# Top-32 attention with two expert layers on one Trainium2 core: transposes and weighted sums of attention weights moved one step later

## Chip, cores and metric

One core of one Trainium2 chip runs the whole program. The metric is device time in microseconds (us). Engines: TensorE (PE; its weight loads PEld), VectorE (DVE), ScalarE (ACT), GpSimd (POOL), and SyncE (SP), whose queue issues most DMAs.

## The reference

Attention over 4 batches, 8 heads, 576 positions, 64 channels keeps the 32 largest scores of each row; its output feeds a gated layer and then a layer of 8 experts, of which each token takes one.

```python
scores = scale * np.matmul(q, k.transpose(0, 1, 3, 2))
kth = np.partition(scores, -top_k, axis=-1)[..., -top_k:-top_k + 1]
scores = np.where(scores >= kth, scores, -1000000000.0)
attn = np.exp(scores - np.max(scores, axis=-1, keepdims=True))
attn = attn / (np.sum(attn, axis=-1, keepdims=True) + 1e-09)
x = np.matmul(attn, v)                       # then to (2304, 512)
h = x @ w_in;  x = (h * np.clip(h + 3, 0, 6) / 6) @ w_out
# each token: expert = argmax(x @ w_gate), weight = its softmax
out[mask] = gate_w[mask, None] * (np.maximum(xe @ w1[e], 0.0) @ w2[e])
```

## The kernel before

The work of attention is cut into T = 144 tiles of up to 128 query rows of one head. Two heads form a pair (p); a visit is the rows of one part of a batch (b) for one pair. A full tile is (head, j); two of them, head 0 and head 1 of the same rows, share a buffer of exponentials. Where a part ends with 64 rows, both heads' 64 rows make one short tile "T", with a buffer of its own; there are 16.

One loop runs over steps t = 0 to T + 5. Each step works on several tiles at once, each at another stage:

- `qk(t + LA)` and `sevac(t + LA)`: scores into PSUM (sps) and their copy by ScalarE into one of five `sbuf`.
- `top_a(t)`: VectorE finds the 32 largest of each row, by maxima of eight blocks (cd), then rounds of maxima (m) and replacements (cw).
- `top_c(t - 1)`, `act_exp(t - 1)`, `act_sign(t - 1)`, `top_z(t - 1)`: the exponentials on ScalarE into `pbuf[pairs[t] % NPB]` (NPB = 2), a count by signs (jk, sg), and a masked copy of the scores (z) on VectorE.
- `mask(t - 2)`: a maximum of z (L646), the match j (L650) that gives the threshold, then the multiplication of the exponentials with the mask (L654, "the mask" below). For a short tile GpSimd then moves and clears columns (L246, L659, L660).
- `trans(t - 3)`, `tevac(t - 3)`: TensorE transposes the masked weights into the PSUM tile `ptps` (L670; the fifth, of the last 64 positions of both heads, L672), ScalarE copies them to SBUF (L248, pt), with one buffer for head 0 (pta, PTA = 1) and one for head 1 and short tiles (ptb, PTB = 1).
- `pv(t - 4)`, `xevac(t - 4)`: TensorE multiplies with the values (L704), also into `ptps`, once for the two heads; VectorE inverts the sums of weights (rs, L717), ScalarE scales (xp, L722). A step later `xt` transposes the result for the next layer (L740, xh, xl). When the last one of a block of 256 rows is done, `blkready` rises.
- `moe_step()`: one of 16 steps of a block in the gated layer (a gated step), if its block is ready: products of layer one (l1ps, L778), gf on ScalarE and VectorE (L784, L790), gh and gl on GpSimd, sums of layer two (yps, L809). `gate_step()` works off the choice of experts of a finished block; its matmuls and a read of counts (lex, L869) use `ptps` too. Conversions of the weights are spread over the first 35 steps or so.

The order on each engine is made by a planner: an instruction gets the due time `pr0 + PRIO[name]` in force when it was written, pr0 rises by STEP = 400 a step, and among those whose inputs the planner's own clock has ready the earliest due goes first. Dependences follow the order of writing; accesses to one PSUM tile by different engines are kept in that order even where their columns differ. Of use here, each within a step: pv −40, qk 10, trans 210, l2 260, l1 310, xevac 440, tevac 450, mask 55, match 560, exp −295, load −1940. The tile `ptps` also holds the small tables `psum_isum`, which the match reads, and `psum_iota`. Loads of values (`load_v`) for visit n + 2 are written once the sums of visit n are, and go through SP's queue.

Behind the loop the remaining steps of the gated layer run alone; then the second expert layer follows, weights streamed from memory.

Of the kernel before, what the change touches and what calls it, by code (L numbers as in the profile page):

```python
# [28 lines left out]
AGE = 0  # L29
KB = 1  # L30
LA = 2
PTA = 1
PTB = 1
SPOOL = 0
TPOOL = 0
WPOOL = 0
# [12 lines left out]
    tevac=450, xt1=-1170, l2=260, sign=175, epi_c=1010, wo=1175, prep=105, top8=270, rounds=-815, epi_b=165, l1=310,  # L49
# [5 lines left out]
def attention_two_moe_kernel(  # L55
# [64 lines left out]
    T = len(tiles)  # L120
# [4 lines left out]
    NV = len(visits)  # L125
    vlast = {n: t for t, (n, o) in enumerate(tiles)}
# [8 lines left out]
    def pr(name):  # L135
        tc.cur_priority = max(0, pr0[0] + PRIO[name])

    def run(gen):
        for _ in gen:
            pass  # L140
# [54 lines left out]
    def body(cs, exact):  # L195
# [45 lines left out]
        def mod(t, n):  # L241
            return (t * n) % 16 < n

        def copy(pool, dst, src):
            if pool:
                G.tensor_scalar(dst, src, 1.0, 0.0, op0=ALU.mult, op1=ALU.add)  # L246
            else:
                A.activation(dst, src, AF.Copy)  # L248
# [83 lines left out]
        conv_load()  # L332


        NPB, NSB, VB = 2, 3 + LA, 2


        pbuf = [ap1.tile([P, 2 * S], F32, name=f"pbuf{i}") for i in range(NPB)]
# [25 lines left out]
        kdone, qdone, kloaded, qloaded, vloaded = [0], [0], [0], [0], [0]  # L364


        def rows(h):
            return slice(h * D, (h + 1) * D)
# [76 lines left out]
        def loads(t):  # L445
            pr("load")
            while kloaded[0] < len(kjobs) and kloaded[0] < kdone[0] + KB + (pjob[0] is not None and pjob[0][0] == "k"):
                b, p = kjobs[kloaded[0]]
                kn = ap1.tile([P, NFC, 2, D], F32, tag="kn", bufs=KB, name=f"kn{b}_{p}")
                kt_ = ap1.tile([TAIL, 2, D], F32, tag="kt", bufs=KB, name=f"kt{b}_{p}")  # L450
                for h in range(2):
                    s = k[b, 2 * p + h]
                    SP.dma_start(kn[:, :, h, :], mains(s))
                    SP.dma_start(kt_[:, h, :], s[N4:S, :])
                kraw[b, p] = (kn, kt_)
                kage[kloaded[0]] = t
                kloaded[0] += 1
            while qloaded[0] < NV and qloaded[0] <= qdone[0] and (pjob[0] is None or pjob[0][0] != "q"):
                n = qloaded[0]
                b, p, q0, w, first = visits[n]  # L460
                qraw[n] = ap1.tile([P, 2, 2, 2, D], F32, tag="qn", bufs=1, name=f"qn{n}")
                nf = w // P
                for h in range(2):
                    s = q[b, 2 * p + h]
                    for j in range(nf):
                        SP.dma_start(qraw[n][:, j, h],
                                     s[q0 + j * P:q0 + (j + 1) * P, :].unsqueeze(1).to_broadcast([P, 2, D]))
                    if w % P:
                        SP.dma_start(qraw[n][0:TAIL, nf, h],
                                     s[q0 + nf * P:q0 + w, :].unsqueeze(1).to_broadcast([TAIL, 2, D]))  # L470
                qage[qloaded[0]] = t
                qloaded[0] += 1

        def load_v():
            pr("load")
            n = vloaded[0]
            vbuf[n] = (vtile[n % VB], vtail[n % VB])
            for h in range(2):
                s = v[visits[n][0], 2 * visits[n][1] + h]
                SP.dma_start(vbuf[n][0][:, h, :, 0:D], mains(s))  # L480
                SP.dma_start(vbuf[n][1][h * TAIL:(h + 1) * TAIL, h, 0:D], s[N4:S, :])
            vloaded[0] += 1
# [181 lines left out]
        def trans(t):  # L664
            pr("trans")
            pb = ts[t]["pb"]
            o = tiles[t][1]
            c0 = SW if o != "T" and o[0] else 0
            for c in range(NFC):
                PE.transpose(ptps[:, c * P:(c + 1) * P], pb[:, c0 + c * P:c0 + (c + 1) * P], ident)  # L670
            if o == "T" or o[0]:
                PE.transpose(ptps[:, N4:SW], pb[:, N4:SW], ident)  # L672

        def tevac(t):
            pr("tevac")
            d = ts[t]
            o = tiles[t][1]
            if o == "T" or o[0]:
                d["pt"] = ap1.tile([P, SW], F32, tag="ptb", bufs=PTB, name=f"pt{t}")
                copy(mod(t, TPOOL), d["pt"], ptps[:, 0:SW])  # L680
            else:
                d["pt"] = ap1.tile([P, N4], F32, tag="pta", bufs=PTA, name=f"pt{t}")
                copy(mod(t, TPOOL), d["pt"], ptps[:, 0:N4])


        def pv(t):
            n, o = tiles[t]
            if o != "T" and o[0] == 0:
                return
            pr("pv")  # L690
            pt = ts[t]["pt"]
            vn, vp = vbuf[n]
            x2 = xps.rearrange("p (h d) -> p h d", h=2)
            mm = [(x2, pt[:, N4:SW], vp)]
            for c in range(NFC):
                cs_ = slice(c * P, (c + 1) * P)
                if o == "T":
                    mm.append((x2, pt[:, cs_], vn[:, :, c, :]))
                else:
                    mm.append((x2[:, 0, :], ts[t - 1]["pt"][:, cs_], vn[:, 0, c, :]))  # L700
            if o != "T":
                mm += [(x2[:, 1, :], pt[:, c * P:(c + 1) * P], vn[:, 1, c, :]) for c in range(NFC)]
            for i, (d_, a_, b_) in enumerate(mm):
                PE.matmul(d_, a_, b_, start=(i == 0), stop=(i == len(mm) - 1))  # L704

        xp = {}
        xtq = []
        blkready = [0]

        def xevac(t):  # L710
            n, o = tiles[t]
            if o != "T" and o[0] == 0:
                return
            pr("xevac")
            x2 = xps.rearrange("p (h d) -> p h d", h=2)
            r = ap1.tile([P, 2], F32, tag="rs", bufs=2, name=f"rs{t}")
            V.tensor_scalar(r, x2[:, :, D], 1e-9, None, op0=ALU.add)  # L717
            V.reciprocal(r, r)
            j = o if o == "T" else o[1]
            xp[n, j] = ap1.tile([P, P], F32, tag="xp", bufs=2, name=f"xp{n}_{j}")  # L720
            for h in range(2):
                A.activation(xp[n, j][:, rows(h)], x2[:, h, 0:D], AF.Copy, scale=r[:, h:h + 1])  # L722
            del ts[t]
            if o != "T":
                del ts[t - 1]
            xtq.append((n, j, t))
            if t == vlast[n]:
                del vbuf[n]
# [236 lines left out]
        def pfin():  # L965
            pnext()
            yield
# [20 lines left out]
            qk(t)  # L988
            sevac(t)
        cacc = 0  # L990
        for t in range(T + 6):
            pr0[0] = pbase + t * STEP
            loads(t)
            while vloaded[0] < NV and (vloaded[0] < VB or vlast[vloaded[0] - VB] <= t - 5):
                load_v()
            ms = moe_step()
            next(ms, None)
            if 0 <= t - 3 < T:
                trans(t - 3)
            if 0 <= t - 1 < T:  # L1000
                top_c(t - 1)
                act_exp(t - 1)
            if t + LA < T:
                ensure(t + LA)
                qk(t + LA)
            if 0 <= t - 4 < T:
                pv(t - 4)
            if t + LA < T:
                sevac(t + LA)
            if 0 <= t - 4 < T:  # L1010
                xevac(t - 4)
            xg = None
            if xtq and (xtq[0][2] < t - 4 or t >= T):
                xg = xt(*xtq.pop(0))
                next(xg)
            if 0 <= t - 3 < T:
                tevac(t - 3)
            if xg:
                next(xg)
            next(ms, None)  # L1020
            if 0 <= t - 1 < T:
                act_sign(t - 1)
            next(ms, None)
            pj = t < T and xg is None and pstart(t + LA)
            if pj:
                pnext()
                if pjob[0] is not None:
                    pnext()
            cacc += CRATE
            others = [ms, mask(t - 2)]  # L1030
            while cacc >= 16:
                cacc -= 16
                others.append(conv_next())
            if xg:
                others.append(xg)
            if pj and pjob[0] is not None:
                others.append(pfin())
            if t < T:
                top_a(t, chain(*others))
            else:  # L1040
                run(chain(*others))
            if 0 <= t - 1 < T:
                top_z(t - 1)
            gate_step()
# [239 lines left out]
```

## Time and profile before

| | us |
|---|---|
| median of 3 runs | 1306.36 (1302.1 to 1306.69) |
| the profiled execution | 1308.57 |
| its span, first to last instruction | 1306.4 |
| busy: TensorE, weight loads | 1168.6, 1034.4 |
| busy: VectorE | 975.4 |
| busy: ScalarE, GpSimd | 820.6, 344.1 |
| mean granted clock of TensorE | 0.941 |

Busy times are shares of an average over unlike stages: loop steps with weight conversions, loop steps with the gated layer, the gated layer alone, the second expert layer. What a change in the loop is worth is read in the stage where it lies, from the waits there. Matmuls are pipelined, so a busy TensorE is not one at its peak.

### The profile page before, as it was taken

The page shows a single profiled execution, that of the slowest core. Times are in us where ns is not written, and L with a number is a line of the kernel's source. Part 1 is how long each engine was busy: PE and PEld are TensorE (multiplying, and loading weights), DVE is VectorE, ACT ScalarE, POOL GpSimd, SP SyncE. Part 2 cuts the span into 40 slices and gives each one's busy share as a digit, 9 for nine tenths or more (in the row PEclk, how much of TensorE's full clock was granted, in tenths as well). Part 3 has the DMA queues.
Part 4 walks back from the last instruction along what each step waited for, and adds up shares of the span by engine and source line. Part 5 has one row for each costly group of instructions (what it writes and reads, how often), then busy time and mean ns, then how long its engine had stood idle before and what let it go on. Part 6 is the DMA issues. An engine that isn't in the chain of part 4 may idle for free.

```text
span 1306.4 us, 23615 instructions
## 1 busy us (share of the span) xinstructions
PE 1168.6 (89%) x7253; PEld 1034.4 (79%) x7253; DVE 975.4 (75%) x3882; ACT 820.6 (63%) x2087; POOL 344.1 (26%) x578
## 2 busy tenths in 40 slices
PE   4577688899999999999999899999985999999995
PEld 3466576788889988888878789898874899999894
DVE  5999999988898999998998798999432444444420
ACT  4777867767688777777777677787432444444421
POOL 1232345421232321221322222322343122222100
PEclk9985589989899999999999899999997999999998
DMA  5444465544444555543543354644684455455400
GB/s 139 132 134 134 122 205 188 166 150 121 130 118 121 140 154 143 135 133 105 128 138 100 92 146 126 135 124 131 217 245 126 135 171 169 152 170 162 135 19 25
DMA packets 184664, 180.20 MB, mean 138 GB/s; under 512 B 123933, under 2 KB 148813, under 8 KB 184528
## 3 DMA queue, kind: packets, MB, share of 16 engines
q1 hardware_dynamic: 180112, 167.52, 44.6%
q0 software_dynamic: 4416, 11.08, 2.6%
q8 instruction: 60, 0.98, 0.3%
q14 instruction: 76, 0.62, 0.2%
HBM read 160.52 MB, written 19.59 MB: 138 GB/s over the span
## 4 chain that ended last, share of the span: by engine, by line
PE 61%; DVE 23%; ACT 8%; DMA 3%; issue 3%; SPq 1%; POOL 1%; ACTq 0%; POOLq 0%; DVEq 0%
PE l1ps L778 10%; PE lp L1119 10%; PE ops L1136 10%; PE yps L809 9%; PE ptps L704 9%; DVE pbuf L654 4%; PE sps L556 4%; PE ptps L670 4%; DVE z L619 3%; DVE cd L586 3%; DVE z L646 3%; DVE m L592 2%; DVE cw L597 2%; ACT pt L248 1%; PE ptps L837 1%
## 5 line engine op out<-in xcount | busy, mean ns | idle before, releaser
L809 PE MATMUL yps<-wo,gh 128*128 128x512 f32 x576 | 214.0, 416 | 3.9 <-DMA wo<-wod 3.4
L778 PE MATMUL l1ps<-xh,wih 128*128 128x256 f32 x576 | 174.1, 302 | 15.5 <-DVE gf L790 12.6
L586 DVE MAX8 cd<-sbuf 128x8 f32<-128x72 f32 x1152 | 183.8, 218 | 2.3 <-ACT sbuf L248 1.9
L246 POOL TENSOR_SCALAR gh<-gf 128x256 fp32r<-128x256 f32 x144 | 64.9, 450 | 414.0 <-DVE gf L790 170.1
L778 PE MATMUL l1ps<-xl,wih 128*128 128x256 f32 x576 | 167.5, 291 | 0.0
L778 PE MATMUL l1ps<-xh,wil 128*128 128x256 f32 x576 | 167.3, 290 | 0.0
L704 PE MATMUL ptps<-vn,pt 128*128 128x65 f32 (+1 forms) x1152 | 156.8, 294 | 0.0
L704 PEld LDWEIGHTS ptps<-vn,pt 128*128 128x128 f32 x1152 | 154.0, 214 | 0.0
L927 DVE TENSOR_TENSOR wl<-raw,wh 128x1024 fp32r<-128x1024 f32 x64 | 78.7, 1233 | 98.1 <-ACT wh L926 98.1
L670 PE MATMUL ptps<-ident,pbuf 128*128 128x128 f32 x576 | 99.3, 297 | 40.2 <-DVE pbuf L654 30.3
L778 PEld LDWEIGHTS l1ps<-xh,wih 128*128 128x128 f32 x576 | 113.0, 196 | 26.6 <-DVE gf L790 19.9
L619 DVE SCALAR_TENSOR_TENSOR z<-sbuf,uall 128x576 f32<-128x576 f32 x144 | 132.9, 923 | 0.4 <-ACT uall L610 0.4
L654 DVE SCALAR_TENSOR_TENSOR pbuf<-sbuf,tall,pbuf 128x576 f32<-128x576 f32 x144 | 124.9, 868 | 0.1
L809 PEld LDWEIGHTS yps<-wo,gh 128*128 128x128 f32 x576 | 108.7, 192 | 19.5 <-issue 4.5
L670 PEld LDWEIGHTS ptps<-ident,pbuf 128*128 128x128 f32 x576 | 70.5, 151 | 65.9 <-ACT jk L636 14.3
L926 ACT ACTIVATE wh<-raw 128x1024 fp32r<-128x1024 f32 x64 | 67.6, 1060 | 87.2 <-PE lp L1119 38.2
L627 ACT ACTIVATE pbuf<-sbuf,nb 128x576 f32<-128x576 f32 x144 | 110.9, 773 | 17.9 <-PE ptps L672 15.9
L809 PE MATMUL yps<-wo,gl 128*128 128x512 f32 x288 | 118.6, 412 | 0.8 <-POOL gl L798 0.8
L784 ACT ACTIVATE gf<-l1ps,three 128x256 f32<-128x256 f32 x144 | 68.1, 473 | 75.4 <-PE l1ps L778 63.9
L778 PEld LDWEIGHTS l1ps<-xl,wih 128*128 128x128 f32 x576 | 113.1, 196 | 2.7
L636 ACT ACTIVATE jk<-sbuf,uall 128x576 bf16<-128x576 f32 x144 | 111.9, 777 | 3.2
L778 PEld LDWEIGHTS l1ps<-xh,wil 128*128 128x128 f32 x576 | 113.2, 196 | 0.1
(178 smaller groups left out, 2957.3 us busy)
## 6 DMA issues: line engine op xcount, KB each, us to landing
wo<-wod SPq DMA_DIRECT2D x144, 512.0 KB
raw<-in_moe_w_dram SPq DMA_DIRECT2D x64, 512.0 KB
vn<-in_v_dram SPq DMA_DIRECT2D x96, 128.0 KB
rawi<-in_moe_w_in_dram SPq DMA_DIRECT2D x16, 512.0 KB
rawo<-in_moe_w_out_dram SPq DMA_DIRECT2D x16, 512.0 KB
qn<-in_q_dram SPq DMA_DIRECT2D x128, 64.0 KB
wod<-wc SPq DMA_DIRECT2D x16, 512.0 KB
yd<-y SPq DMA_DIRECT2D x18, 258.0 KB
```

Source lines behind the costliest of these rows:

```text
L586: V.max(cd[:, c, :], s[:, c * CK:(c + 1) * CK])
L619: V.scalar_tensor_tensor(d["z"], s, d["u"], s, op0=ALU.is_le, op1=ALU.mult)
L627: A.activation(d["p"], d["s"], AF.Exp, bias=d["nb"], scale=SCALE)
L636: A.activation(jk, d["s"][:, 0:S], AF.Sign, bias=ts[t]["u"], scale=-1.0, accum_out=d["sg"])
L654: V.scalar_tensor_tensor(d["p"], d["s"], tall[:, t:t + 1], d["p"], op0=ALU.is_ge, op1=ALU.mult)
L670: PE.transpose(ptps[:, c * P:(c + 1) * P], pb[:, c0 + c * P:c0 + (c + 1) * P], ident)
L704: PE.matmul(d_, a_, b_, start=(i == 0), stop=(i == len(mm) - 1))
L778: PE.matmul(dst, a[:, c, fs], b_[:, c, :], start=(n == 0), stop=(n == 3 * NCC - 1))
L809: PE.matmul(yps[tt], a[:, tsl], b_, start=(f == 0 and m == 0), stop=(f == NF1 - 1 and m == 2))
L927: V.tensor_tensor(l, raw, r_(h), op=ALU.subtract)
L1119: PE.matmul(lp, a[:, c, fs], b_[:, c, :], start=(n == 0), stop=(n == 3 * NCC - 1))
L1136: PE.matmul(ops_[j], a[:, js], b_[:, ns], start=(f == 0 and m == 0), stop=(f == NF2 - 1 and m == 2))
```

## The change

Transposes and weighted sums of a tile are written one step later: `trans` and `tevac` work on tile t − 4, `pv` and `xevac` on t − 5. Due times within a step are the same. The loop has one more turn. The loads of values and the transposes of results (`xt`) follow by one step. There are three buffers of exponentials and two of each kind of transposed weights.

```diff
-PTA = 1
-PTB = 1
+PTA = 2
+PTB = 2
...
-        NPB, NSB, VB = 2, 3 + LA, 2
+        NPB, NSB, VB = 3, 3 + LA, 2
...
-        for t in range(T + 6):
+        for t in range(T + 7):
             pr0[0] = pbase + t * STEP
             loads(t)
-            while vloaded[0] < NV and (vloaded[0] < VB or vlast[vloaded[0] - VB] <= t - 5):
+            while vloaded[0] < NV and (vloaded[0] < VB or vlast[vloaded[0] - VB] <= t - 6):
                 load_v()
             ms = moe_step()
             next(ms, None)
-            if 0 <= t - 3 < T:
-                trans(t - 3)
+            if 0 <= t - 4 < T:
+                trans(t - 4)
             if 0 <= t - 1 < T:
                 top_c(t - 1)
                 act_exp(t - 1)
             if t + LA < T:
                 ensure(t + LA)
                 qk(t + LA)
-            if 0 <= t - 4 < T:
-                pv(t - 4)
+            if 0 <= t - 5 < T:
+                pv(t - 5)
             if t + LA < T:
                 sevac(t + LA)
-            if 0 <= t - 4 < T:
-                xevac(t - 4)
+            if 0 <= t - 5 < T:
+                xevac(t - 5)
             xg = None
-            if xtq and (xtq[0][2] < t - 4 or t >= T):
+            if xtq and (xtq[0][2] < t - 5 or t >= T):
                 xg = xt(*xtq.pop(0))
                 next(xg)
-            if 0 <= t - 3 < T:
-                tevac(t - 3)
+            if 0 <= t - 4 < T:
+                tevac(t - 4)
```

## Rows read from the trace of the kernel before

**Rows 1.** Busy us by stage: PE, PEld, DVE, ACT, POOL; granted clock, DMA share, GB/s.
```profile
0.00:160.00 160.00, 96.86 (x390) 79.80 (x391) 140.06 (x539) 110.27 (x276) 43.27 (x58) 0.78 0.47 134
160.00:276.00 116.00, 99.40 (x604) 84.49 (x605) 106.37 (x396) 80.42 (x214) 52.76 (x76) 0.90 0.55 172
276.00:916.00 640.00, 614.30 (x4336) 549.91 (x4335) 580.55 (x2693) 484.88 (x1364) 161.54 (x319) 0.98 0.47 129
```

**Rows 2.** The same view, instructions of line 619 (z, one a tile) on DVE alone.
```profile
276.00:916.00 640.00, 90.77 (x109) 0.98 0.47 129
765.00:916.00 151.00, 23.66 (x28) 1.00 0.47 126
```

**Rows 3.** Busy us as in rows 1, of two other stretches.
```profile
765.00:916.00 151.00, 148.77 (x1086) 135.26 (x1085) 137.92 (x646) 115.51 (x319) 40.11 (x68) 1.00 0.47 126
1100.00:1200.00 100.00, 100.00 (x518) 90.51 (x518) 44.31 (x54) 43.77 (x63) 20.03 (x27) 1.00 0.51 160
```

**Rows 4.** Time line, 820 to 822 us: start, us, engine, line, out<-in [idle before <-releaser].
```profile
820.19 0.23 DVE L650 SCALAR_TENSOR_TENSOR j<-ptps,sg,z 128x16 f32<-128x16 f32 x1 [0.33 <-ACT pt L248]
...
820.47 0.82 DVE L654 SCALAR_TENSOR_TENSOR pbuf<-sbuf,tall,pbuf 128x576 f32<-128x576 f32 x1
...
821.43 0.63 PE L670 MATMUL ptps<-ident,pbuf 128*128 128x128 f32 x4
...
821.90 0.39 PE L704 MATMUL ptps<-vp,pt 128*128 128x130 f32 x2
```

**Rows 5.** Busy us by stage, instructions of line 790 (gf) on DVE alone.
```profile
160.00:276.00 116.00, 6.16 (x15) 0.90 0.55 172
...
920.00:985.00 65.00, 7.08 (x17) 0.97 0.78 238
```

**Rows 6.** Waits of PE, 276 to 916 us: who waited for whom: us, times, longest.
```profile
PE ptps L670 <- DVE pbuf L654: 5.2, 15, 0.7
PE ptps L670 <- DVE lex L869: 4.5, 4, 1.9
PE ptps L672 <- DMA qn<-in_q_dram: 3.2, 1, 3.2
...
PE ptps L672 <- POOL pbuf L659: 0.9, 1, 0.9
```

**Rows 7.** Time line around one short tile, 734 to 739 us.
```profile
734.00 0.24 POOL L246 TENSOR_SCALAR pbuf<-pbuf 64x64 f32<-64x64 f32 x1 [4.37 <-DMA td<-tok,ad]
...
734.51 0.47 PE L672 MATMUL ptps<-ident,pbuf 128*128 128x128 f32 x1 [3.24 <-DMA qn<-in_q_dram]
...
738.76 0.16 DVE L717 TENSOR_SCALAR rs<-ptps 128x2 f32<-128x2 f32 x1 [6.19 <-PE ptps L704]
```

**Rows 8.** Busy us as in rows 1, the two stretches behind it.
```profile
735.00:740.00 5.00, 5.00 (x22) 4.71 (x22) 1.24 (x7) 2.31 (x6) 0.14 (x1) 0.50 0.02 5
740.00:745.00 5.00, 5.00 (x24) 4.58 (x22) 3.24 (x15) 1.97 (x7) 1.52 (x4) 0.63 0.33 105
```

**Rows 9.** Waits of PE, 0 to 160 us.
```profile
PE ptps L670 <- DVE pbuf L654: 25.2, 12, 4.9
```

**Rows 10.** Waits of DVE, 0 to 160 us and 160 to 276 us.
```profile
DVE rs L717 <- PE ptps L704: 2.9, 2, 1.4
...
DVE rs L717 <- PE ptps L704: 3.6, 2, 2.0
```

**Rows 11.** Waits of all engines, 276 to 916 us.
```profile
POOL pbuf L660 <- PE ptps L672: 15.6, 8, 6.1
ACT pbuf L627 <- PE ptps L672: 10.6, 15, 3.6
DVE j L650 <- ACT pt L248: 7.2, 22, 0.6
```

**Rows 12.** Waits of SP's DMA queue, 276 to 916 us.
```profile
SPq L764 <- PE yps L809: 212.6, 71, 8.9
...
SPq L481 <- PE ptps L704: 31.1, 22, 5.1
```

## Prediction

> **What bounds the kernel now.** I read first the busy time of each engine stage by stage [rows 1], with the number of tiles [rows 2]. Up to 160 us tiles pass without steps of the gated layer (gated steps below); VectorE is busy 140.06 of 160 us, TensorE 96.86, so VectorE sets the pace. From 160 to 276 us they carry the last weight conversions and the first of those steps: VectorE 92%. From 276 to 916 us 109 tiles pass with one such step each, 5.87 us a tile; here both are close to full, TensorE 614.30 of 640 us and VectorE 580.55. Behind 916 us there is no attention left. The change acts on the first three stages and, by one more loop turn, on the fourth; the expert layer behind it, up to the end of the span, it doesn't touch.
>
> In the third stage TensorE idles 640 − 614.30 = 25.7 us, and its granted clock is 0.98, which costs about another 13 us. This is all that TensorE could ever give back there. In the stretch from 765 to 916 us, where hardly a stall is left, 28 tiles take 151 us, 5.39 each [rows 2, 3]: the floor that the stage has when nothing goes wrong.
>
> By the busy share of matmuls TensorE is at 98.5% in that stretch, by that of weight loads at 89.6%; from 1100 to 1200 us, where matmuls never pause (100.00 of 100 us), the weight loads stand at 90.5% [rows 3]. So 89.6% is as full as this engine gets here. The Trainium skill ("Perfetto Trace Analysis", Identifying the Most-Contended Engine) says that matmul occupancy is no good measure of the room left and that the busy share of weight loads is one; read so, a tenth of the stage would be free, and the third rival below is what would follow.
>
> Then the waits. Which wait does the change aim at? In step t the transposes are those of tile t−3, the mask is that of t−2: a tile's transposes come one step after its mask. One pass in the time line [rows 4]: the match (j) starts at 820.19 us, released by the copy of transposed weights (pt), the mask at 820.47, the transposes at 821.43, and the weighted sum is queued right behind them. So each step holds a ring: transposes, copy, match, mask, transposes of the next tile.
>
> **The change part by part.** No operation is added or removed; the 144 tiles keep their transposes, copies and sums. What moves is when they may start.
>
> *(a) One more loop turn.* The gated steps of a block start when its last weighted sum is transposed, so all start one turn later, and the loop has T+7 turns. One turn in the VectorE-bound stages loses its gated step, worth 0.41 us of VectorE there (6.16 us for 15 multiplications of gf); one more turn with a gated step alone is run behind the attention: 65 us for 17 of them, 3.8 us [rows 5]. Sum +3.4 us. Ends: 0, if that turn fits into idle time behind 916 us; 7.7 us, a whole turn of the second stage (116 us for 15 of them).
>
> *(b) TensorE's waits in the third stage.* The transposes wait for the mask 15 times, 5.2 us in all, and for GpSimd's part of the mask of a short tile (T) in 2 places, 3.2 and 0.9 us [rows 6]. The 3.2 us carry a DMA's name, but the time line shows what it was [rows 7]: GpSimd stood 4.37 us behind an indirect DMA of its own, copied the short tile's columns only at 734.00 us, and the fifth transpose started at 734.51. The granted clock then stood at 0.50 (1.2 GHz throughout) and 0.63 in the next two stretches of 5 us [rows 8], so some 4.3 us more were lost, and VectorE too stood still for 6.19 us, for the sum behind the transpose. With a whole step (5.9 us) between mask and transposes both kinds of wait go. I count the event in full, 3.2 + 4.3 + 0.9 = 8.4 us, as no engine worked through it; the mask's 5.2 us I count by half, 2.6, since VectorE at 91% is next in line. Sum −11.0 us. Ends: −13.6 (all) and 0 (VectorE takes everything back).
>
> *(c) The first two stages.* Here the transposes wait for the mask 25.2 us in 12 places [rows 9]; that is worth nothing itself, since VectorE is the bound and TensorE has 63 us free there [rows 1]. What counts is that VectorE waits for the weighted sums that are queued behind: 2.9 + 3.6 us [rows 10]. A sum no longer held behind the mask comes up to a step earlier in relation to it; I take half, −3 us, as the engine does other work meanwhile only in part. Ends −6.5 and 0.
>
> *(d) Three buffers of exponentials.* An exponential is written over those of two pairs before, once they are transposed; ScalarE waits 10.6 us for those transposes in the third stage, GpSimd 15.6 us for the clearing of a short tile's columns [rows 11]. With three buffers and transposes a step later, an even tile's exponential needs transposes issued two steps before it instead of one. Both waits shrink. ScalarE is 76% busy and GpSimd 25% [rows 1], so I take 0; ends −10.6 and 0.
>
> *(e) Two buffers of each kind of transposed weights.* With the sums as many steps behind the copies as before, the second buffer lets a copy go ahead of the sum that still reads the first; that is a wait of a copy for a sum, and the views of waits have none. 0; as an upper end the whole of ScalarE's wait before the exponentials, which (d) holds already.
>
> *(f) Loads.* The values of visit n+2 are asked for one step later, as are the sums that free their buffer and those that need them; the distance stays. On SP's queue these loads (31.1 us of waiting for sums before those of the tail rows) move past one load of second-layer weights (wo), and wo waits 212.6 us for its own buffers in this stage, 3.0 us each time [rows 12]: what passes was waiting anyway. 0; if that cover failed in one place, TensorE would stand for one such wait, 3.0 us.
>
> *(g) What stays in the ring.* The match reads a table that shares a PSUM tile with the transposes: it waits for the copy 22 times, 7.2 us in the third stage [rows 11]; the transposes wait for another VectorE read of it (lex, a gate's) 4 times, 4.5 us [rows 6]. These orders hold after the change too: transposes, copy, match, transposes. Only the mask (0.82 us in the pass above) leaves the ring; match, copy and transposes stay [rows 4]. As transposes arrive earlier at that point, more of them will meet lex or the match: I take half of the 4.5 us once more, +2.3; ends 0 and what the second rival makes of it.
>
> Sum: 3.4 − 11.0 − 3.0 + 2.3 = −8.3 us. The profiled execution took 1308.57 us (span 1306.4), 2.2 above the median of the runs; the difference is taken to that median, 1306.36: 1298.1, so **1298 us**, with 1291 to 1301 as its own range.
>
> **The rivals.** *First, the gain stays small:* VectorE is the next bound, 5.3 us of work a tile (580.55/109) against 5.87 us [rows 1, 2], and the ring through the PSUM tile still closes once a step. Then only half of (b)'s event comes back, 4 us, against +3.4: about 1305 us. For it speaks that the mask's waits in stage three are short, 0.35 us on average, and that the big one is a single event. The Trainium skill ("PSUM — Partial Sum Buffer", PSUM bank collisions raise a hardware error) says that two engines must not touch one bank at once, reads against reads included, so such an order of copy and match has to be kept; the 22 waits agree.
>
> *Second, slower:* the order of each engine's instructions is made anew by due times. Transposes are due at 210, ahead of the sums of layer two (260) and the products of layer one (310). Until now they were held back by the mask and those matmuls went first. Now nothing but the match or lex holds them, so they can be set ahead of that work, and at run time TensorE, which is in order, waits for VectorE with it queued behind. At the mean of today's waits, 0.35 us, at every second tile that is 54 × 0.35 = 19 us: about 1317 us. It decides from 8.3/109 = 0.08 us a tile. Against it: before, the same place costs only 0.05 us a tile (5.2/109).
>
> *Third, a larger gain:* it is the ring and not the engines that sets 5.87 us a tile, and with 0.82 us out of it half of TensorE's 25.7 + 13 us comes back instead of (b)'s 11: 1298 − 8 = 1290, down to 1280 if more does. Against it stands the clean stretch, 5.39 us a tile with the ring as it is.
>
> **How the numbers follow.** Forecast 0.38, first rival 0.31, second 0.20, third 0.11. The forecast's own range holds its bounds of (a) to (c) near the middle; for 8 in 10 the range goes from 1284 (most of the third) to 1315 (most of the second). About 0.5%, 6.5 us, is what a measurement can tell from no change: below 1299.8 lie the third rival and most of the forecast, 0.46; between, the first and the forecast's edge, 0.35; above 1312.9 the second, 0.19.
>
> **What would show it.** Right: no wait of transposes for the mask and none for GpSimd's clearing; ScalarE's wait before the exponentials near 0; gated steps starting some 7 us later; one more lone gated step, 3 to 4 us, behind the attention; 109 tiles in 630 us or less. Wrong: as much waiting of the transposes for the match or lex as there was for the mask (second rival); VectorE's busy share in the third stage over 95% with no gain (first); a stage of 620 us or less (third).

## The result and the profile after

The changed kernel takes 1293.5 us (1290.71 to 1293.98 in 5 runs) against 1306.36 (1301.7 to 1309.84): a ratio of 0.9891 [0.9864, 0.9918], 12.9 us less where 8.3 were forecast. The profiled spans, 1290.9 and 1306.4, differ by 15.5. A second comparison gave 0.9905 (e12, below).

After, busy time by the stages of [rows 1], same columns; the stages now end a little earlier:

```profile
0.00:160.00 160.00, 87.25 (x386) 71.59 (x387) 144.65 (x541) 109.86 (x274) 41.51 (x58) 0.85 0.47 130
160.00:276.00 116.00, 101.48 (x634) 88.61 (x632) 112.05 (x428) 87.33 (x231) 53.21 (x78) 0.89 0.61 193
276.00:916.00 640.00, 620.17 (x4446) 554.14 (x4446) 578.34 (x2686) 486.79 (x1365) 171.09 (x328) 1.00 0.48 132
```

In the third stretch the granted clock is 1.00 where it was 0.98. But fixed stretches no longer hold the same work, so from here on I cut by tiles: from the start of one z (line 619) to that of another, 20 and 35 being its number. The first stage is then z0 to z20, the second z20 to z35, the third z35 to z143, and behind z143 stand the last gated steps. In us:

| | z0–z20 | z20–z35 | z35–z143 | z143 to the last gf | gf behind z143 |
|---|---|---|---|---|---|
| before | 135.5 | 114.7 | 638.9 | 72.2 | 21 |
| before, second profile (e11) | 134.5 | 114.2 | 637.6 | 71.5 | 21 |
| after | 135.3 | 105.0 | 624.0 | 81.6 | 22 |
| after, second profile (e12) | 135.3 | 105.0 | 623.4 | 81.3 | 22 |

The two profiles of each kernel agree within 1.5 us in every stage. They are two executions each, though: other executions of the kernel before went from 1295.1 to 1310.7 us on one chip, so a few us of a stage can be the execution's own. Between the first two profiles the gain is 9.7 us in the second stage and 14.9 in the third, and 9.4 are given back behind the attention; expert layer and first stage stay.

Before, the second and the third stage, cut by tiles (columns as in rows 1):

```profile
162.00:276.70 114.70, 98.10 (x602) 83.19 (x601) 104.70 (x393) 79.16 (x213) 52.15 (x75) 0.90 0.56 175
276.71:915.61 638.90, 613.20 (x4325) 548.81 (x4325) 579.82 (x2692) 484.37 (x1361) 161.40 (x318) 0.98 0.47 129
```

After, the same two:

```profile
161.40:266.40 105.00, 91.05 (x562) 79.19 (x561) 102.24 (x390) 78.10 (x209) 50.83 (x74) 0.88 0.60 190
266.37:890.34 623.97, 603.68 (x4330) 539.35 (x4330) 576.44 (x2688) 485.42 (x1361) 163.06 (x317) 1.00 0.49 132
```

In the second stage VectorE's work is nearly the same (104.70 and 102.24 us); its idle time falls from 10.0 us to 2.8. In the third the number of matmuls is the same (4325, 4330), but two things fell: TensorE's idle time from 638.90 − 613.20 = 25.7 us to 20.3, and its *busy* time from 613.20 to 603.68. With equal work, less busy time goes here with a higher granted clock, 1.00 against 0.98. So of the 14.9 us I count 9.5 as clock and 5.4 as waits.

The waits after, beside [rows 6, 11] (who waited for whom: us, times, longest), TensorE first, then all engines, 276 to 916 us:

```profile
PE ptps L670 <- DVE lex L869: 4.4, 5, 2.0
PE ptps L670 <- DVE j L650: 1.9, 5, 0.6
...
POOL pbuf L660 <- PE ptps L672: 18.0, 7, 5.5
DVE j L650 <- ACT pt L248: 13.1, 28, 1.0
...
ACT pbuf L627 <- PE ptps L672: 2.3, 5, 0.6
```

No transposes wait for the mask (pbuf, L654) or for GpSimd's clearing any more. ScalarE's wait ahead of the exponentials went from 10.6 to 2.3 us. GpSimd's wait for its clearing did not shrink (15.6, now 18.0) and costs nothing. The transposes wait 6.3 us for lex and the match, 4.5 before, and the match's wait for the copy grew from 7.2 to 13.1 us. Of VectorE's wait for the sums (rs, L717), 17.4 us before in the third stage cut by tiles, 1.6 are left.

### The profile page after: what moved, and what is told of

The parts are those of the page before. It is cut to its first block, busy times and chain, and to the rows that moved or that the text cites. A ratio compares the mean times of both kernels' runs of the same rounds, so it can differ in the third digit from the quotient of the medians.

```text
span 1290.9 us, 23533 instructions
## 1 busy us (share of the span) xinstructions
PE 1148.2 (89%) x7253; PEld 1017.9 (79%) x7253; DVE 976.0 (76%) x3882; ACT 821.9 (64%) x2087; POOL 345.8 (27%) x578
## 4 chain that ended last, share of the span: by engine, by line
PE 60%; DVE 9%; ACT 4%; DMA 3%; issue 2%; POOL 0%; SPq 0%; POOLq 0%; ACTq 0%; DVEq 0%
PE l1ps L778 11%; PE lp L1119 10%; PE ops L1136 10%; PE yps L809 10%; PE ptps L704 7%; PE sps L556 4%; PE ptps L670 3%; DVE pbuf L654 1%; DVE cd L586 1%; PE ptps L837 1%; DVE z L646 1%; PE tp L1101 1%; DVE z L619 1%; DVE cw L597 1%; PE misc L414 1%
## 5 line engine op out<-in xcount | busy, mean ns | idle before, releaser
L809 PE MATMUL yps<-wo,gh 128*128 128x512 f32 x576 | 209.6, 411 | 1.2 <-DMA wo<-wod 0.8
L704 PE MATMUL ptps<-vn,pt 128*128 128x65 f32 (+1 forms) x1152 | 146.6, 282 | 0.0
L704 PEld LDWEIGHTS ptps<-vn,pt 128*128 128x128 f32 x1152 | 143.4, 201 | 0.0
L654 DVE SCALAR_TENSOR_TENSOR pbuf<-sbuf,tall,pbuf 128x576 f32<-128x576 f32 x144 | 126.2, 877 | 0.1
L670 PE MATMUL ptps<-ident,pbuf 128*128 128x128 f32 x576 | 97.9, 295 | 21.5 <-DVE j L650 14.9
L248 ACT ACTIVATE sbuf<-sps 128x576 f32<-128x576 f32 x144 | 93.1, 647 | 37.2 <-PE sps L556 22.1
L798 POOL TENSOR_TENSOR gl<-gf,gh 128x256 fp32r<-128x256 f32 x144 | 112.5, 782 | 11.4
```

Of the source, the lines that this page charges most:

```text
L654: V.scalar_tensor_tensor(d["p"], d["s"], tall[:, t:t + 1], d["p"], op0=ALU.is_ge, op1=ALU.mult)
L798: G.tensor_tensor(gl, gf, r_(gh), op=ALU.subtract)
L809: PE.matmul(yps[tt], a[:, tsl], b_, start=(f == 0 and m == 0), stop=(f == NF1 - 1 and m == 2))
```

## The experiments

Ratios are to the kernel before on the same chip, with 95% intervals. None of the versions is faster than the change beyond the noise. Stage lengths of a version come from one profile of it.

**The buffers alone** (e1), and **the change without the second buffers of transposed weights** (e2):

```diff
-PTA = 1
-PTB = 1
+PTA = 2
+PTB = 2
...
-        NPB, NSB, VB = 2, 3 + LA, 2
+        NPB, NSB, VB = 3, 3 + LA, 2
```

e2 is the changed kernel with PTA = PTB = 1.

> Three buffers of exponentials and two of each kind of transposed weights, but transposes and sums at their old steps. Theory (the gain is that the transposes no longer stand behind the mask): nothing of that changes, so 1306 +- 4 us, with ScalarE's wait before the exponentials (L627, 10.6 us in the third stage before, 2.3 after) near 0 and VectorE's wait for the sums (rs, 17.4 us) as before. Rival (the gain comes from the buffers): 1296 us or less, rs waits down to some 5 us.

> The change with single buffers of transposed weights (three of exponentials). Theory: the second buffers do nothing, since a copy comes behind the sum that read the buffer anyway: 1293 +- 4 us. Rival (they carry part of the gain, by letting a copy go ahead of a sum): 1300 us or more, and copies (pt, L248) that wait for sums (L704).

e1: 1305.87 us, 1.0001 [0.9978, 1.0023]. e2: 1292.0 us, 0.9894 [0.9864, 0.9924], the change's own ratio. Buffers without later steps bring nothing: in e1 ScalarE's wait ahead of the exponentials falls from 10.6 to 2.0 us, and the time stays. Of the later steps, nothing hangs on the second copies of the weights. Later transposes with only two buffers of exponentials were not run.

**Only the sums later** (e3): transposes stay at t−3, weighted sums and what follows them move to t−5, so the loop gets its extra turn.

```diff
-PTA = 1
-PTB = 1
+PTA = 2
+PTB = 2
...
-        for t in range(T + 6):
+        for t in range(T + 7):
...
-            if 0 <= t - 4 < T:
-                pv(t - 4)
+            if 0 <= t - 5 < T:
+                pv(t - 5)
...
```

> Only the weighted sums one step later (two buffers of each kind of transposed weights, two of exponentials); transposes stay one step behind the mask. Theory (transposes behind the mask are the cost): the waits of L670 for L654 and of L672 for GpSimd stay, the gated steps still start a turn later: 1304 to 1312 us. Rival (the cost was that sums stood right behind transposes and copies, and VectorE behind the sums): 1297 us or less, with rs waits under 6 us in the third stage.

1296.62 us, 0.9922 [0.9891, 0.9952]: most of the gain without moving a transpose. Its transposes do wait for the mask in the third stage (waits of TensorE and VectorE, 276 to 900 us):

```profile
PE ptps L670 <- DVE pbuf L654: 4.5, 8, 1.3
...
DVE rs L717 <- PE ptps L704: 10.0, 15, 2.0
```

The 5.2 us of [rows 6] are still nearly all there and the kernel is still faster, so the expected 1304 to 1312 us was wrong. The time is the rival's (1297 or less); its sign is not, as VectorE waits 10.0 us for the sums and not under 6. Most of the gain can be had with the mask's wait in place; what that wait is worth, e9 and e10 show below.

**Only the gated steps later** (e5). In e3 and in the change the gated steps start one turn later too, since a block is ready when its last sum is transposed. Here that alone is done: the count of ready blocks is seen one turn late.

```diff
...
-            if g >= NG + 3 or (g < NG and blkready[0] <= g // NF1):
+            if g >= NG + 3 or (g < NG and blkseen[0] <= g // NF1):
...
-        for t in range(T + 6):
+        for t in range(T + 7):
...
+            blkseen[0], blkprev[0] = blkprev[0], blkready[0]
...
```

A block's last products can here read rows of the next block but one, written into the same buffer, so its output isn't the reference's; the work done is the same.

> Steps of transposes, sums and buffers as before; only the gated steps see a finished block one turn later, and the loop has one more turn. It is the cost of the change without its gain. Theory (sums later bring the gain, the extra turn costs): 1306 + 3 to + 9 us, 1309 to 1315, with the stretch behind the last tile's z longer by 4 to 9 us (72.2 before, 81.6 after the change). Rival (the second stage is faster because the first gated step comes later, 114.7 us before and 105.0 after for 15 tiles): that stretch falls to 107 us or less here too, and the time stays at 1303 to 1309 us.

1298.99 us, 0.9976 [0.9948, 1.0004]. The second stage is no shorter (116.4 us), the third, cut by tiles, is as short as the change's:

```profile
278.02:902.00 623.98, 604.56 (x4325) 540.03 (x4324) 574.54 (x2688) 482.58 (x1361) 162.01 (x316) 1.00 0.45 132
```

And this with the transposes still waiting for the mask (waits of TensorE, 276 to 900 us):

```profile
PE ptps L670 <- DVE pbuf L654: 4.7, 13, 1.0
```

The expected loss (1309 to 1315 us) did not come, nor the rival's shorter second stage. In the third stage, by the profile, the place of the gated steps alone does what the whole change does; VectorE still waits 9.9 us there for the sums. How much of that the time shows is less clear: the profiled spans of e5 and of before (on another chip) differ by 9.0 us, the medians on e5's chip (1298.99 and 1302.49) by 3.5, and the interval of the ratio holds no change at all.

**The change, and e3, with the gated steps where they were** (e9, e10). The attention results are transposed in the turn of their sum, so blocks are ready at the old turn. The edit is to the change, for e10 the same to e3:

```diff
-        for t in range(T + 7):
+        for t in range(T + 6):
...
-            if xtq and (xtq[0][2] < t - 5 or t >= T):
+            if xtq and (xtq[0][2] < t - 4 or t >= T):
```

> The change with the transposes of results (xt) in the step of their sum instead of the step behind it: a block is ready as early as before, the gated steps keep their old place beside the tiles and the loop its T+6 turns. Theory (the extra turn costs, the distance between mask, transposes and sums gains): 1293.5 less 3 to 8 us, 1285 to 1290, second stage 105 us for 15 tiles, stretch behind the last tile's z 72 to 77 us. Rival (the third stage is faster because the gated steps lie one tile further back, as in the run where they alone were moved): the third stage goes back to 635 us and the time to 1297 to 1302.

> Only the sums one step later (as in the run with that label), with the transposes of results in the step of their sum, so that gated steps and the number of turns are as before. If the distance of the sums is what gains: 1289 to 1295 us, second stage 107 us. If the place of the gated steps was the gain: 1302 us or more.

> The kernel before once more, for a second profile. If the 114.7 us of the second stage and the 638.8 of the third are the kernel's own, both come back within 3 us; if the single event at a short tile (some 8 us at 731 us) was chance, the third stage is 631 us here.

> The changed kernel once more, on the chip of the run without the extra turn, for the comparison of the two: 1291 to 1296 us, second stage 105 us, third 624, the stretch behind it 81 us.

e9: 1296.77 us, 0.9949 [0.9926, 0.9972]. e10: 1306.92, 1.0018 [0.9996, 1.0039]. On their chip the change once more (e12): 1293.28, 0.9905 [0.9878, 0.9933]; the kernel before once more (e11): 1305.96, with the stages shown above: both came back, within what was expected. e9 lies between what was expected of it and its rival (third stage 629.8 us, second 105.4 as expected); e10 is the second of its two cases, no gain without the gated steps' new place. As a table of two things:

| ratio | gated steps as before | one turn later |
|---|---|---|
| transposes and sums as before | 1 | 0.9976 (e5) |
| sums later | 1.0018 (e10) | 0.9922 (e3) |
| transposes and sums later | 0.9949 (e9) | 0.9891, 0.9905 |

So about half of the gain hangs on the turn in which the gated steps start, which the forecast held only as a cost: on one chip e9 keeps 0.0051 of e12's 0.0095. With the sums alone later that turn is worth about 1%, with nothing else moved 0.24%, not clear of noise. e9 and e10 also bring the transposes of the attention result a turn nearer to their sum, which costs 2.4 us of TensorE's waits in e9's third stage against 1.5 in after; a small part of the difference may be that.

The table read downwards prices the step that the change was made for. e10 and e9, on one chip, differ by the transposes alone (and the third buffer of exponentials): 1306.92 and 1296.77 us, intervals apart. In e10 the transposes still wait in the third stage (waits of TensorE, 276 to 900 us), in e9 neither wait is left, and TensorE's idle time there goes from 26.8 to 18.4 us:

```profile
PE ptps L672 <- POOL pbuf L659: 3.7, 5, 1.6
...
PE ptps L670 <- DVE pbuf L654: 2.2, 5, 1.4
```

Where the gated steps have moved already (e3 to the change) the same step is worth only 0.2 to 0.3%, not clear of noise. The two parts of the change do not simply add.

**The third stage in all kernels**, cut by tiles. Falls: places where the granted clock falls below 1.00, read in stretches of 5 us, without the stage's last 5 us.

| gated steps | kernel | us | busy | idle | falls |
|---|---|---|---|---|---|
| as before | before | 638.9 | 613.2 | 25.7 | 4 |
| | e11, before again | 637.6 | 611.9 | 25.7 | 4 |
| | e1 | 637.2 | 609.9 | 27.3 | 2 |
| | e4 (below) | 635.4 | 610.0 | 25.4 | 3 |
| | e6 (below) | 638.8 | 615.2 | 23.6 | 3 |
| | e9 | 629.8 | 611.4 | 18.4 | 3 |
| | e10 | 636.1 | 609.3 | 26.8 | 2 |
| later | after | 624.0 | 603.7 | 20.3 | 0 |
| | e12, after again | 623.4 | 603.5 | 19.9 | 0 |
| | e2 | 626.1 | 606.6 | 19.5 | 1 |
| | e3 | 629.1 | 605.5 | 23.6 | 1 |
| | e5 | 624.0 | 604.6 | 19.4 | 1 |
| | e7 (below) | 624.9 | 605.0 | 19.9 | 0 |
| | e8 (below) | 623.0 | 603.5 | 19.5 | 0 |

The busy times of the two groups do not overlap: 609.3 to 615.2 against 603.5 to 606.6. In e9 the idle time is 7.3 us below that of before, with no transposes waiting for a mask, and the busy time is that of before. But e5, whose transposes do wait for the mask, has as little idle time (19.4): there it fell because other waits of TensorE fell, lex (4.5 to 0.6 us) and the short tiles. The number of falls is that of one profile of each kernel, and for before and after of two.

What falls look like in before, three of the four (the fourth is [rows 7, 8]); columns as in rows 1:

```profile
311.00:316.00 5.00, 4.21 (x27) 3.98 (x27) 3.99 (x20) 3.52 (x12) 0.09 (x1) 0.76 0.27 59
316.00:321.00 5.00, 5.00 (x33) 4.52 (x32) 4.02 (x16) 4.29 (x13) 1.58 (x5) 0.89 0.31 102
346.00:351.00 5.00, 3.40 (x17) 3.43 (x18) 3.85 (x22) 2.58 (x6) 2.81 (x6) 0.68 0.74 198
351.00:356.00 5.00, 5.00 (x28) 4.83 (x27) 2.13 (x15) 1.94 (x7) 0.00 (x0) 0.64 0.01 3
681.00:686.00 5.00, 3.15 (x16) 1.98 (x15) 4.79 (x18) 4.39 (x14) 0.49 (x3) 0.97 0.76 232
686.00:691.00 5.00, 5.00 (x28) 4.34 (x28) 3.14 (x17) 1.72 (x7) 1.38 (x4) 0.69 0.26 70
```

First TensorE stands still for a part, then it is busy throughout while the granted clock shows that a part of the time went at 1.2 GHz, the lower of its two levels. What it had stood for, in before's time line:

```profile
312.34 1.06 PE L837 MATMUL ptps<-wg,yt 128*128 128x8 f32 x8 [0.79 <-DVE j L650]
...
347.61 0.94 PE L670 MATMUL ptps<-ident,pbuf 128*128 128x128 f32 x4 [1.87 <-DVE lex L869]
...
683.90 0.41 PE L829 MATMUL misc<-ident,y 128*128 128x128 f32 x2 [1.17 <-DVE kx L389]
```

All three are of the gate: its product (L837), its read of the PSUM table that it shares with the transposes (lex), its transposes (L829) behind the preparation of the next head's keys (kx) in the tile misc. None is the wait for a mask. In e9 a fall follows on a pause behind the key preparation, too (two stretches, and the time line in the first):

```profile
461.00:466.00 5.00, 2.36 (x12) 1.56 (x12) 4.74 (x17) 4.76 (x14) 0.09 (x1) 0.97 0.60 181
466.00:471.00 5.00, 5.00 (x25) 5.00 (x24) 4.30 (x22) 0.83 (x3) 1.47 (x2) 0.50 0.26 59
...
465.24 0.41 PE L414 MATMUL misc<-ident,qn 128*128 128x128 f32 x2 [1.69 <-DVE kx L402]
```

A pause is not always followed by a fall. TensorE's waits in e7, which has no fall in this stage, hold a longer one of the same kind (270 to 900 us):

```profile
PE misc L393 <- DVE kx L389: 2.4, 1, 2.4
```

What the runs show is the number of falls and its price: against the 603.5 us of e12, (613.2 − 603.5)/4 = 2.4 us each in before, (611.4 − 603.5)/3 = 2.6 in e9, 3.9 in e6 and 2.2 in e4. e6 and e4 have three falls each and the same mean granted clock, 0.98, and 5.2 us between their busy times, so busy time holds more than the clock, and a price of this kind is good to a few us. That moving the gated steps against the tiles changes which pieces of the gate, the key preparation and the short tiles meet, and so the number of long pauses, is argued from the rows above; which meeting brings a fall isn't settled.

**Short tiles without GpSimd** (e6, old steps): copying and clearing their columns goes to the other engines.

```diff
-                copy(True, hi[TAIL:P], lo[TAIL:P])
-                G.memset(lo[TAIL:P], 0.0)
-                G.memset(hi[0:TAIL], 0.0)
+                copy(False, hi[TAIL:P], lo[TAIL:P])
+                V.memset(lo[TAIL:P], 0.0)
+                V.memset(hi[0:TAIL], 0.0)
```

> The kernel before with a short tile's columns moved by ScalarE and cleared by VectorE in place of GpSimd: its 16 masks no longer queue behind GpSimd's indirect DMAs. If the short tiles' wait for GpSimd carries the gain of their two regions (tiles 32 to 47 and 97 to 111), 1298 to 1302 us, with no wait of L672 for GpSimd and the 15 steps from tile 97 at 92 us (97.6 before, 91.4 after). If it was one unlucky event of one profile: 1304 to 1309 us.

1304.98 us, 1.0016 [0.999, 1.0042]. The event of [rows 7] is gone, as are the transposes' waits for GpSimd, but the stage is as long (638.8 us): the waits went on elsewhere, with three falls of the clock at other places. The 15 steps from tile 97 take 96.4 us, not the 92 that were expected. In its waits of TensorE (276 to 906 us) and its time line:

```profile
PE ptps L670 <- DVE pbuf L654: 7.1, 16, 1.8
...
319.37 0.25 PE L393 MATMUL misc<-ident,kt 64*128 64x64 f32 x1 [0.61 <-DVE kx L389]
...
445.57 0.24 PE L393 MATMUL misc<-ident,kt 64*128 64x64 f32 x1 [1.76 <-DVE kx L389]
```

**The ring cut at another place** (e4, old steps): the match reads the copy of its table in SBUF, not the PSUM tile that the transposes write, so it no longer waits for the copy of weights.

```diff
-                V.scalar_tensor_tensor(j8, psum_isum, d["sg"], ...
+                V.scalar_tensor_tensor(j8, isum, d["sg"], ...
```

> The kernel before with the match reading its table from SBUF instead of from the PSUM tile of the transposes; steps and buffers as before. So the match no longer waits for the copy, nor the transposes for the match. If the ring transposes, copy, match, mask is what costs, cutting it here gives most of the change's gain without its extra turn: 1293 to 1298 us, with L670 waiting for the mask under 2 us in the third stage. If the mask's nearness alone costs, L670 waits for the mask as before (5.2 us) and the time stays 1303 to 1309 us.

1309.59 us, 1.0021 [0.9999, 1.0043]. Cutting the link between copy and match, the one that stays after the change, brings nothing to the whole: the third stage is 3.5 us shorter, the first two together 6.5 longer, for a reason that stays open. The transposes' wait for the mask, 3.8 us, lies between the two signs. This kernel still has the event of the short tile, at the same place as [rows 7], this time under its own name:

```profile
734.53 0.47 PE L672 MATMUL ptps<-ident,pbuf 128*128 128x128 f32 x1 [4.01 <-POOL pbuf L659]
```

**Two turns later** (e7): transposes at t−5, sums at t−6, four buffers of exponentials, T+8 turns.

```diff
-        NPB, NSB, VB = 3, 3 + LA, 2
+        NPB, NSB, VB = 4, 3 + LA, 2
...
-        for t in range(T + 7):
+        for t in range(T + 8):
...
-            if 0 <= t - 4 < T:
-                trans(t - 4)
+            if 0 <= t - 5 < T:
+                trans(t - 5)
...
```

> The change made once more: transposes on tile t-5, sums on t-6, four buffers of exponentials, T+8 turns. Theory (one step frees the sums for good, every further turn only costs): 1293.5 + 3 to + 9 us, 1296 to 1303. Rival (the gain grows with distance): 1290 us or less.

1299.89 us, 0.9991 [0.9964, 1.0019], as the theory had it. Its profiled execution has the second and third stage of the change (105.8 and 624.9 us) and 84.2 us with 23 steps of gf behind z143. That execution took 1297.42 us, 2.5 under the median and 4.7 over the profiled one of the change, so it shows only a part of where the gain goes. The rest stays open.

**The stretch behind the attention** (e8, on the change): the first expert's weights are split a turn after they were asked for, so that ScalarE, with the next gf queued behind the split, does not stand waiting for their DMA.

```diff
+            wraw.append((e, i, raw))
+
+        def wpiece_split():
+            e, i, raw = wraw.pop(0)
...
-                wpiece(0, pre[-1])
+                wpiece_load(0, pre[-1])
```

The reason was these rows of after's time line:

```profile
949.03 1.06 ACT L926 ACTIVATE wh<-raw 128x1024 fp32r<-128x1024 f32 x1 [4.19 <-DMA raw<-in_moe_w_dram]
949.99 0.46 ACT L784 ACTIVATE gf<-l1ps,three 128x256 f32<-128x256 f32 x1
...
951.73 0.39 PE L778 MATMUL l1ps<-xh,wih 128*128 128x256 f32 x1 [2.88 <-DVE gf L790]
```

> The change, and behind the loop the splitting of the expert layer's first weights on ScalarE and VectorE is written one turn after its load instead of at once. In the profile after, ScalarE stands at such a splitting (L926) for its load, with gf queued behind it, and TensorE waits 2.9 and 3.9 us for gf. If that is what makes the stretch behind the last tile 9.4 us longer instead of 3.8, 1285 to 1290 us and no wait of l1ps for gf over 1 us there; if the order only shifts the wait elsewhere, 1292 to 1296 us.

1293.95 us, 0.9932 [0.9912, 0.9952], and 83.6 us behind z143, not less. The edit did not remove the pause: TensorE waits 5.3 us for gf there, 6.8 in after. But these waits do not follow the stretch's length over the kernels: 3.7 us in the 72.2 of before, 3.9 in e9's 77.2, 4.2 in e12's 81.3. So the pause is not what makes the stretch long.

## Why the prediction was right, step by step

The time, 1293.5, lies within the range and on the forecast's side, 4.6 us below it, near the lower edge of the forecast's own range (1291). The signs were right and three terms were too small. That the sum still came near is partly luck, as the errors go both ways: 6.2 us too little gain in the third stage ((b) and (g)) and 6.7 in the second, 6.0 too little loss behind them.

**(a), one more turn: the size of the step right, the sum too small.** The lone gated step costs 81.3 − 77.2 = 4.1 us (e12 against e9, 22 gf against 21) and 75.4 − 72.2 = 3.2 (e5 against before); 3.8 was forecast. But the stretch grew by 9.4. The other part appears in e9 as well, which has no extra turn: 77.2 against 72.2, 5 us. Attention work of the last tiles (transposes, sums, results) moves behind z143 with the later steps, and some of it isn't covered. The forecast held nothing for that; its upper end, 7.7, was passed. VectorE's 0.41 us less in the second stage can't be told apart.

Before, the stretch from the end of the attention on (columns as in rows 1):

```profile
916.00:992.00 76.00, 71.93 (x455) 62.32 (x453) 26.12 (x71) 26.61 (x56) 28.64 (x50) 0.98 0.70 218
```

After, the same:

```profile
891.00:976.00 85.00, 78.12 (x496) 68.09 (x495) 28.27 (x79) 28.08 (x60) 31.12 (x55) 0.96 0.62 196
```

TensorE issues 496 matmuls there where it issued 455, and idles 6.9 us where it idled 4.1.

**(b), the third stage: the named waits went, the clock was mis-sized, the cause only half seen.** Of the forecast's 11.0 us, 3.2 + 0.9 + 2.6 = 6.7 were idle time; less (g)'s 2.3, that is 4.4, and 5.4 was measured. The clock's part was 4.3; 9.5 was measured. The first part of the prediction had the whole price in hand, a granted clock of 0.98 worth 13 us, but counted the one fall that lay behind a short tile. The other three lay behind the gate, which the change moves as well. I had followed the gated steps only to the end of the loop, where their extra turn costs, and not to where they now lie beside the tiles. That the event of the short tile goes was right; that it is worth its 8.4 us was not shown: e6 removes it, and the stage is as long as before. That the waits for mask and GpSimd cost time is borne out by e10 and e9, where moving the transposes alone takes 8.4 us of idle time out of this stage. But in the change itself they can't be given the 5.4 us: e5 leaves the transposes where they were and has the same stage, 624.0 us, by the gated steps' place alone. So the forecast's size here rests in part on something that it did not hold.

**(c), the first two stages: mechanism right, size too small.** The forecast took 3 us, with 6.5 as the end; 9.7 came, all in the second stage. VectorE's waits for sums there were 3.6 us in 2 places [rows 10]; after has none left among VectorE's waits there (160 to 266 us):

```profile
DVE xl L754 <- ACT xh L750: 1.0, 1, 1.0
...
DVE j L650 <- ACT pt L248: 0.3, 1, 0.3
```

Its idle time fell by 7.2 us, though, and its work by 2.5. The end was set by the listed waits for the sums alone; VectorE's other waits listed there fell as well, from 5.3 us to 2.3. That a late sum held these too is argued, and why the work fell is not known. Kernels with later sums need 103 to 110 us for these 15 tiles, those without 112 to 118, e5 (116.4) among them: it is the later sums, not the gated place. In the first stage, as was said, the mask's 25.2 us were worth nothing: they turned into other waits of an engine with time to spare, and the stage is as long.

After, TensorE's waits from 0 to 160 us, beside [rows 9]:

```profile
PE misc L740 <- ACT xp L722: 26.4, 8, 5.6
PE ptps L670 <- DVE j L650: 11.3, 6, 3.9
```

**(d), (e): right in price.** Nothing by themselves (e1, e2); but GpSimd's wait, which (d) said would shrink, grew. **(f): right**: TensorE's waits for second-layer weights (wo) fell, from 3.4 us to 0.8. **(g): small, as taken.** The transposes' waits for lex and match grew by 1.8 us; 2.3 were taken.

**The rivals.** The first, that the gain stays small as the ring through the PSUM tile closes in any case, fell with the time itself: e4 cuts that link and the whole gains nothing, and VectorE's share in the third stage, 576.44 of 624.0 us or 92%, is not at its end. The second, slower, fell: where transposes are no longer held by the mask they wait for match or lex in 10 places, 6.3 us in all, not at every second tile. The third, a gain of 16 to 26 us, comes nearer in size for the third stage (16.7 us with (g), where 14.9 were measured) but for another reason: what came back was mostly clock behind single pauses, not a ring of every step. Its reading of the weight loads rests on the Trainium skill ("Perfetto Trace Analysis", Identifying the Most-Contended Engine), which takes their busy share, and not that of matmuls, as the measure of how close TensorE is to its limit. Read as room up to 100%, it isn't borne out here: they stand at 90.5% where matmuls never pause [rows 3], and at 86.4% in after's third stage (539.35 of 623.97), where matmuls take 96.7%.

**What was named to look for.** Seen: no waits for mask or clearing; 624 us for the third stage; ScalarE's wait down to 2.3 us, not quite to 0; one more lone step of 3 to 4 us; gated steps later, the first gf at 169.6 us instead of 164.8, 5 us and not 7.

## What to carry to other kernels

When a stage of one stream moves, everything that is started by its end moves too: price the other stream's new place, not only its extra turn at the end. Where an engine's granted clock is below 1.00 in a stage that counts, find every place where it falls and what the engine had stood for, and give each its part of the price, before one event is taken for the whole. A move that starts work later pays at the drain: look at what the last items leave behind the loop, beside the extra turn itself.

## What the runs showed of the hardware

Pauses of TensorE of 0.8 to 3.2 us were followed in before by up to 10 us in which it was busy without a break at a granted clock between 0.50 and 0.89. With its four falls the busy time of the third stage is 9.5 us longer than after, more than the idle time that went from that stage (5.4). The falls repeat at the same places in both profiles of before (311, 346, 681 and 731 us). But the pause of 2.4 us in e7 passed without a fall, and which pauses bring one could not be read from these runs.
